# Weights ahead of v, key copies on GpSimd, and v windows by parity in a fused attention and MLP kernel

## The chip, the cores and the metric

One core of one Trainium2 chip runs the whole program. The metric is the device time in microseconds (us) of one execution, median of several. TensorE is called PE in the profile, VectorE DVE, ScalarE ACT, GpSimd POOL, SyncE SP.

## The reference

Attention of 2 batches, 8 heads, 768 positions, head width 64, in which each query sees the keys within 15 positions and, in addition, 24 block summaries (the maximum of 32 keys, the mean of 32 values). Two MLPs (512 to 2048 to 512) follow on the 1536 tokens:

```python
k_sum = k.reshape(B, H, nb, block, D).max(axis=3)
v_sum = v.reshape(B, H, nb, block, D).mean(axis=3)
scores_l = np.where(abs(pos_i - pos_j) < window, scale * q @ k.T, -1e9)
scores_s = scale * q @ k_sum.T + log(block)
a = softmax(concatenate([scores_l, scores_s], -1))
x = a @ concatenate([v, v_sum])
# tokens x 512, then
h = x @ w_in;  x = (max(h, 0) + alpha * min(h, 0)) @ w_out
h = x @ w_in2; out = (h / (1 + exp(-h))) @ w_out2
```

## The kernel before

**Attention** runs in 24 groups: 6 blocks of 256 queries (`blk`, three to a batch) times 4 pairs of heads (`p`). The first eight groups alternate between blocks 0 and 1 over the pairs (groups 0 and 1 are pair 0, groups 2 and 3 pair 1, and so on), then come blocks 2 to 5. Each pair of each batch has a key tile `kT` (for each 128 queries the 160 keys around them, with 24 free columns in front of each piece), the whole of v (`y<-in_vT` for batch 0, `raw<-in_vT` for batch 1), and the tile `vs`, the v rows of each 64 queries' window below or above 24 rows for the block means. `prep_k` takes the block maxima of the keys on DVE (L329) and copies them into the free columns of the other five pieces (L335). `prep_v1` halves v by two adds on POOL (L346) and reduces it on DVE (L349); `prep_v2` transposes that on PE and spreads it over `vs` on ACT (L359).

A group goes through `scores` (PE L387, then DVE L395 with the mask and L404), `exps` (ACT L412, row sums), `normalize` (DVE L421 and L423, then POOL L424), `turn` (PE transposes L430, ACT L432) and `values` (PE L443, ACT L451, DVE L452), which leaves attention output as a high and a low part, `xh` and `xl`, in fp32r.

**Weights** come in pieces of 128x512 in fp32 (512 KB, stored as pairs of 32-bit words). `load_next` asks for the next piece on the SP queue (L108); `conv_next` assembles the piece by three DVE instructions (L125, L129, L132), and `rest` makes a high part on ACT (L138) and a low part on POOL or DVE (L139). The first three pieces land in the free part of `y`, later ones in one of two staging tiles `raw`, which the v of batch 1 uses too. So piece 5 can be asked for once piece 3 is converted. Pieces 0 to 3 are needed by `first_in`, the first layer for block 0 as its pairs arrive, pieces 4 to 7 by `out_pair`, its second matrix.

**The MLPs** (`in_item`, `out_pair`, `out_item`) run three fp32r products for each fp32 one (L153 to L155). They start among the attention groups and fill the time behind them.

**The order.** All steps of attention, the loads and the first matrix work are put on one list with keys (`at(key, ...)`) and sorted by key: group k has its scores at k, exps at k + 0.1, normalize at k + 0.3, block sums at k + 1.3, turn at k + 1.8, values at k + 3.2. The sorted list is a rank: a planner sets the order of each engine's instructions from it, taking the first in rank among those that it holds to be ready, so the order on an engine departs from the keys. At run time each engine and each queue goes through its order strictly. Loads of the beginning have the key -100 and all go out on SP, in order: kT, q, the constants (identity and masks in one tile, 304 KB), v and the two window halves of pair 0, then the same for the pairs behind it (480, 128, 384 and 2 x 288 KB), with weight pieces 0, 1, 2 and 3 behind groups 3, 4, 5 and 6. The second half of the windows, and the keys and v of batch 1, come later by keys of their own. Conversion n has the key `CONV + n * CONV_STEP`, that is -1.4, -0.8, ... 2.8.

Of the kernel before, what the change touches and what calls it, by code (L numbers as in the profile page):

```python
# [10 lines left out]
F32 = mybir.dt.float32  # L11
# [9 lines left out]
WIN = SUB + 2 * PAD  # L21
P = 128
# [4 lines left out]
AT_EXPS, AT_NORM, AT_TURN, AT_VALUES = 0.1, 0.3, 1.8, 3.2  # L27
AT_IN = 5.3
AT_LATER, ITEM_STEP = 3.5, 0.8
CONV, CONV_STEP = -1.4, 0.6  # L30
CONV2, CONV2_STEP = 14.0, 1.5
BATCH, BATCH_STEP = 5.8, 2.0
NQ = 6
# [4 lines left out]
def tile_blocks_attention_mlps(  # L38
# [7 lines left out]
    w2: bass.AP,  # L46
    alpha: bass.AP,
    consts: bass.AP,
    out: bass.AP,
):  # L50
    nc = tc.nc
    B, NPAIR, _, S = qT.shape
    D = 64
    NB = S // BLOCK
    NSUB = S // SUB
    NC = WIN + NB
    NTWO = S // P
# [3 lines left out]
    NCH, _, CF = w1.shape[:3]  # L61
# [7 lines left out]
    const = ctx.enter_context(tc.tile_pool(name="const", bufs=1))  # L69
# [4 lines left out]
    wp1 = ctx.enter_context(tc.tile_pool(name="wp1", bufs=CF))  # L74
    ps_mm = ctx.enter_context(tc.tile_pool(name="ps_mm", bufs=6, space=bass.MemoryType.PSUM))

    cst = const.tile([P, P + 4 * NC], F32, name="cst")
    ident = cst[:, 0:P]
    mask = cst[:, P:]
    al = const.tile([P, NFF], F32, name="al")  # L80
    nal = const.tile([P, NFF], F32, name="nal")

# [5 lines left out]
    y_w = y.rearrange("p a n -> p (a n)")[:, NPAIR * S:].rearrange("p (a n w) -> p a n w", n=512, w=2)  # L88
# [205 lines left out]
    with ExitStack() as scope0:  # L294

        gpool.append(ctx.enter_context(tc.tile_pool(name="g1", bufs=2)))
        kv = scope0.enter_context(tc.tile_pool(name="kv", bufs=4))
# [11 lines left out]
        def load_v(b, p):  # L309
            if b == 0:  # L310
                t = y_v[:, p]
            else:
                t = stage.tile([P, 512, 2], F32, name="raw").rearrange("p n w -> p (n w)")[:, :S]
            nc.sync.dma_start(out=t, in_=vT[b, p])
            vt_t[b, p] = t
            t = kv.tile([NC, NSUB, P], F32, tag="vs", name="vs")
            vs_t[b, p] = t
            nc.sync.dma_start(out=t[NB:, 0::2], in_=vw[b, p, 0])
            nc.sync.dma_start(out=t[:WIN, 1::2], in_=vw[b, p, 1])

        def load_q(blk, p):
            b, j = divmod(blk, BPB)
# [4 lines left out]
        def prep_k(b, p):  # L327
            t = kt_t[b, p]
            nc.vector.tensor_reduce(  # L329
                out=t[:, 0, :NB].rearrange("p (n m) -> p n m", n=NTWO),  # L330
                in_=t[:, :NTWO, NB + PAD:NB + PAD + P].rearrange("p n (m i) -> p n m i", i=BLOCK),
                axis=AX.X,
                op=ALU.max,
            )
            nc.vector.tensor_copy(  # L335
                out=t[:, 1:, :NB], in_=t[:, 0:1, :NB].to_broadcast([P, NTWO, NB])
            )

# [13 lines left out]
        def prep_v2(b, p):  # L352
            s_ = vs_t[b, p]
            pt = ps_mm.tile([P, 512], F32, tag="mm", name="pv")
            nc.tensor.transpose(pt[:NB, :P], vr_t.pop((b, p)), ident)

            def spread(s0, s1):
                for at in (s_[:NB, 2 * s0:2 * s1:2], s_[WIN:, 2 * s0 + 1:2 * s1:2]):
                    nc.scalar.activation(  # L359
                        out=at,  # L360
                        in_=pt[:NB, 0:P].unsqueeze(1).to_broadcast([NB, s1 - s0, P]),
                        func=AF.Copy,
                        scale=1.0 / BLOCK,
                    )

            spread(0, QB // P)
            return lambda: spread(QB // P, NTWO)
# [3 lines left out]
        def where(n):  # L371
            blk, p = order[n]
            b, j = divmod(blk, BPB)
            return blk, p, b, j
# [60 lines left out]
        def values(n):  # L435
            blk, p, b, j = where(n)
            t, s_ = pt_t.pop(n), vs_t[b, p]
            ps = ps_mm.tile([P, 512], F32, tag="mm", name="o")[:, :QB]
            for i in range(2):
                for s in range(2):  # L440
                    for h in range(2):
                        c = (2 * h + i) * P + s * SUB
                        nc.tensor.matmul(  # L443
                            ps[h * D:(h + 1) * D, i * P + s * SUB:i * P + (s + 1) * SUB],
                            s_[:, 2 * (2 * j + i) + s, h * D:(h + 1) * D],
                            t[:, c:c + SUB],
                            start=True,
                            stop=True,
                        )
            at = slice(blk * QB, (blk + 1) * QB)  # L450
            nc.scalar.copy(out=xh[:, p, at], in_=ps)  # L451
            nc.vector.tensor_tensor(out=xl[:, p, at], in0=ps, in1=xh[:, p, at], op=ALU.subtract)  # L452
# [30 lines left out]
        def at(key, f, *a):  # L483
            ops.append((key, len(ops), f, a))
# [5 lines left out]
        def flush():  # L490
            while loads:
                weights = loads[0] is None
                if not weights or at_load[0] >= y_w.shape[1]:
                    if staged[0] >= (STAGE if weights else STAGE - 1):
                        return
                    staged[0] += 1
                g = loads.pop(0)
                if weights:
                    load_next()
                else:  # L500
                    load_v(*g)
# [6 lines left out]
        first = -100.0  # L508
        for k, (blk, p) in enumerate(order[:2 * NPAIR]):
            if blk == 0:  # L510
                at(first, load_k, 0, p)
            if k < NQ:
                at(first, load_q, blk, p)
            if k == 0:
                at(first, lambda: nc.sync.dma_start(out=cst, in_=consts))
            if blk == 0:
                at(first, load_v, 0, p)
            if NPAIR <= k + 1 <= 2 * NPAIR - 1:
                at(first, ask, None)
        at(first, lambda: nc.sync.dma_start(out=al, in_=alpha))  # L520
        at(first, lambda: nc.gpsimd.tensor_scalar(out=nal, in0=al, scalar1=-1.0, scalar2=None, op0=ALU.mult))
        for _ in range(NPAIR, 2 * CF):
            at(first, ask, None)

        spread_t = {}
# [51 lines left out]
        for k, (blk, p) in enumerate(order):  # L577
            b, j = divmod(blk, BPB)
# [13 lines left out]
            if blk == 0:  # L592
                at(k + AT_IN, first_in, p)
        for n in range(2 * CF):
            at(CONV + n * CONV_STEP, conv_op, n)
        for n in range(CF):
            at(CONV2 + n * CONV2_STEP, conv_op, 2 * CF + n)
        at(NG - 2 * CF + 2.0, more_loads)
        for p in range(NPAIR if B > 1 else 0):
            t = BATCH + p * BATCH_STEP  # L600
            k = idx[BPB - 1, p]
            at(max(t, k + 0.01), load_k, 1, p)
            at(max(t, k + AT_VALUES + 0.01), ask, (1, p))
        t = idx[0, NPAIR - 1] + AT_IN
        for i, *_ in seq:
            if i >= NBLK:
                break
            t = max(t + ITEM_STEP, lastk[i] + AT_LATER)
# [18 lines left out]
def _layout(q, k, v, moe_w_in, moe_w_out, moe_alpha, moe2_w_in, moe2_w_out):  # L627
    B, H, S, D = q.shape
    pad = PAD
    nb, nsub = S // BLOCK, S // SUB  # L630

    def turned(a):
        return np.ascontiguousarray(a.transpose(0, 1, 3, 2).reshape(B, H // 2, 2 * D, S))

    kp = np.zeros((B, H // 2, 2 * D, S + 2 * pad), k.dtype)
    kp[:, :, :, pad:pad + S] = turned(k)
    kT = np.stack([kp[:, :, :, i:i + P + 2 * pad] for i in range(0, S, P)], axis=3)
    vp = np.zeros((B, H // 2, S + 2 * pad, 2, D), v.dtype)
    vp[:, :, pad:pad + S] = v.reshape(B, H // 2, 2, S, D).transpose(0, 1, 3, 2, 4)
    vp = vp.reshape(B, H // 2, S + 2 * pad, 2 * D)  # L640
    vw = np.stack(
        [
            np.stack([vp[:, :, i + odd:i + odd + WIN] for i in range(0, S, P)], axis=3)
            for odd in (0, SUB)
        ],
        axis=2,
    )

    def weights(w_in, w_out):

        dm, dff = w_in.shape
        n = dff // dm
        a = w_in.reshape(dm // P, P, n, dm).transpose(2, 0, 1, 3)
        b = w_out.reshape(n, dm // P, P, dm)
        return np.ascontiguousarray(np.stack([a, b], axis=1)).view(np.uint64)


    m = np.zeros((3, P, WIN + nb), np.float32)
    for t, first in enumerate((0, P, S - P)):
        pos = first + np.arange(P)[:, None]  # L660
        key = first + (np.arange(P)[:, None] // SUB) * SUB - pad + np.arange(WIN)[None, :]
        ok = (np.abs(pos - key) < WINDOW) & (key >= 0) & (key < S)
        m[t] = np.log(BLOCK)
        m[t, :SUB, nb:] = np.where(ok, 0.0, -1000000000.0)[:SUB]
        m[t, SUB:, :WIN] = np.where(ok, 0.0, -1000000000.0)[SUB:]
    consts = np.concatenate(
        [np.eye(P, dtype=np.float32)] + [m[t] for t in (0, 1, 1, 2)], axis=1
    )

    return {  # L670
        "qT": turned(q),
        "kT": np.ascontiguousarray(kT),
        "vT": turned(v),
        "vw": np.ascontiguousarray(vw),
        "w1": weights(moe_w_in, moe_w_out),
        "w2": weights(moe2_w_in, moe2_w_out),
        "alpha": np.ascontiguousarray(moe_alpha.reshape(-1, P).T),
        "consts": np.ascontiguousarray(consts),
    }


# [17 lines left out]
```

## Time and profile before

| | |
|---|---|
| runs | 620.99 us median of 3 (617.88 to 621.72) |
| profiled execution | 619.27 us, span 617.5 us |
| PE busy | 589.0 us, 95% of the span |
| DVE busy | 360.1 us, 58% |
| ACT busy | 261.3 us, 42% |
| POOL busy | 72.7 us, 12% |
| DMA | 52.54 MB, mean 85 GB/s, 31770 packets, 20976 of them under 2 KB |

The profiled execution's 619.27 us are its span and 1.77 us around it. Shares are means over the whole span; the attention with its loads lies in the first 140 us or so, and the rows below are read from there.

### The profile page before, as it was taken

What the parts mean: (1) busy time and instruction counts of PE and PEld (TensorE: products, weight loads), DVE (VectorE), ACT (ScalarE), POOL (GpSimd) and SP (SyncE); (2) the same over time, 40 slices, a digit from 0 to 9 for tenths busy, and PEclk for the clock granted to TensorE, in tenths of its full rate; (3) what the DMA queues carried; (4) which work ended last, traced back from release to release, by engine and by line L of the source; (5) the groups of instructions that cost most, each with busy time, mean ns of one, the idle gap of its engine ahead of it and who ended that gap; (6) DMA issues with size and microseconds to landing.
All of it is one profiled execution on the core that took longest, in us unless ns stands there. A gap on an engine that the chain in (4) does not pass through costs nothing.

```text
span 617.5 us, 8894 instructions
## 1 busy us (share of the span) xinstructions
PE 589.0 (95%) x3476; PEld 492.8 (80%) x3476; DVE 360.1 (58%) x629; ACT 261.3 (42%) x606; POOL 72.7 (12%) x69
## 2 busy tenths in 40 slices
PE   2777999999999999999999999999999999999997
PEld 1565888999888888888888888888888888888886
DVE  3899979549995587449764890067325732222222
ACT  2768977654533433433553553354124213212310
POOL 1657754232000000000000000000000000000000
PEclk9998999999999999999999999999999999999999
DMA  9968844001441034004400231024200300000011
GB/s 246 316 203 258 230 153 137 2 2 69 139 166 37 1 136 137 0 1 136 137 0 1 89 123 62 1 68 137 69 0 31 106 1 1 2 0 36 34 69 68
DMA packets 31770, 52.54 MB, mean 85 GB/s; under 512 B 2288, under 2 KB 20976, under 8 KB 31728
## 3 DMA queue, kind: packets, MB, share of 16 engines
q1 hardware_dynamic: 31728, 51.97, 27.1%
q8 instruction: 27, 0.44, 0.3%
q14 instruction: 15, 0.12, 0.1%
HBM read 48.82 MB, written 3.15 MB: 84 GB/s over the span
## 4 chain that ended last, share of the span: by engine, by line
PE 85%; DVE 8%; DMA 3%; SPq 1%; ACT 1%; issue 1%; POOL 0%; DVEq 0%; POOLq 0%
PE ps L153 28%; PE ps L154 27%; PE ps L155 27%; DVE w L129 1%; DMA y<-in_w 1%; DMA vs<-in_vw 1%; DVE w L132 1%; PE o L443 1%; DVE t L395 1%; DVE nm L404 1%; DVE w L125 1%; DMA raw<-in_w 1%; PE sc L387 1%; DVE kT L329 1%; PE pt L430 1%
## 5 line engine op out<-in xcount | busy, mean ns | idle before, releaser
L153 PE MATMUL ps<-xh,wl 128*128 128x512 f32 (+1 forms) x432 | 159.0, 373 | 0.4 <-ACT xh L451 0.3
L154 PE MATMUL ps<-xl,wh 128*128 128x512 f32 (+1 forms) x432 | 158.7, 368 | 0.0
L155 PE MATMUL ps<-xh,wh 128*128 128x512 f32 (+1 forms) x432 | 158.2, 367 | 0.0
L204 DVE TENSOR_TENSOR gl<-g,gh 128x512 fp32r<-128x512 f32 x84 | 57.6, 690 | 100.8 <-ACT gh L203 100.8
L153 PEld LDWEIGHTS ps<-xh,wl 128*128 128x128 f32 x432 | 81.9, 192 | 14.9 <-issue 1.0
L154 PEld LDWEIGHTS ps<-xl,wh 128*128 128x128 f32 x432 | 82.1, 190 | 13.3 <-issue 0.2
L155 PEld LDWEIGHTS ps<-xh,wh 128*128 128x128 f32 x432 | 82.0, 190 | 13.3
L200 ACT ACTIVATE g<-ps 128x512 f32<-128x512 f32 x48 | 28.7, 598 | 139.0 <-PE ps L155 137.5
L154 PE MATMUL ps<-gl,wh 128*128 128x512 f32 (+1 forms) x240 | 82.9, 348 | 0.0
L155 PE MATMUL ps<-gh,wh 128*128 128x512 f32 (+1 forms) x240 | 82.6, 346 | 0.0
L153 PE MATMUL ps<-gh,wl 128*128 128x512 f32 (+1 forms) x240 | 78.6, 350 | 0.1
L154 PE MATMUL ps<-wl,gh 128*128 128x512 f32 (+1 forms) x196 | 75.4, 385 | 0.0
L153 PE MATMUL ps<-wh,gl 128*128 128x512 f32 (+1 forms) x196 | 74.7, 385 | 0.0
L155 PE MATMUL ps<-wh,gh 128*128 128x512 f32 (+1 forms) x196 | 73.4, 385 | 0.0
L203 ACT CAST gh<-g 128x512 fp32r<-128x512 f32 x96 | 59.6, 622 | 25.9 <-DVE g L195 24.4
L138 ACT CAST wh<-w 128x512 fp32r<-128x512 f32 x64 | 39.2, 623 | 52.4 <-DVE w L132 39.1
L260 DVE TENSOR_TENSOR y<-ps,y 128x512 f32<-128x512 f32 x48 | 32.2, 688 | 48.8 <-PE ps L155 48.8
L195 DVE SCALAR_TENSOR_TENSOR g<-m,nal,g 128x512 f32<-128x512 f32 (+1 forms) x60 | 41.2, 701 | 25.3 <-ACT m L192 25.3
L191 ACT ACTIVATE g<-ps 128x512 f32<-128x512 f32 (+1 forms) x50 | 28.9, 579 | 60.5 <-PE ps L155 57.2
L153 PEld LDWEIGHTS ps<-gh,wl 128*128 128x128 f32 x240 | 45.2, 189 | 6.9 <-issue 0.5
L154 PEld LDWEIGHTS ps<-gl,wh 128*128 128x128 f32 x240 | 45.3, 189 | 6.0 <-POOL gl L204 0.2
L155 PEld LDWEIGHTS ps<-gh,wh 128*128 128x128 f32 x240 | 45.3, 189 | 5.7
(51 smaller groups left out, 684.9 us busy)
## 6 DMA issues: line engine op xcount, KB each, us to landing
raw<-in_w SPq DMA_DIRECT2D x61, 512.0 KB, 3.8
vs<-in_vw SPq DMA_DIRECT2D x16, 288.0 KB, 6.9
kT<-in_kT SPq DMA_DIRECT2D x8, 480.0 KB, 5.0
q<-in_qT SPq DMA_DIRECT2D x24, 128.0 KB, 4.2
out<-s SPq DMA_DIRECT2D x11, 256.0 KB, 2.0
y<-in_vT SPq DMA_DIRECT2D x4, 384.0 KB, 6.9
y<-in_w SPq DMA_DIRECT2D x3, 512.0 KB, 7.8
raw<-in_vT SPq DMA_DIRECT2D x4, 384.0 KB, 5.3
```

The costliest lines, as they stand in the source:

```text
L125: nc.vector.tensor_scalar(out=w, in0=high, scalar1=3, scalar2=0x3FFFFFFF, op0=ALU.logical_shift_left, op1=ALU.bitwise_and,)
L129: nc.vector.scalar_tensor_tensor(out=w, in0=high, scalar=0xC0000000, in1=w, op0=ALU.bitwise_and, op1=ALU.bitwise_or)
L138: nc.scalar.copy(out=hi, in_=w)
L153: nc.tensor.matmul(ps, all_, bh, start=first, stop=False)
L154: nc.tensor.matmul(ps, ah, bl, start=False, stop=False)
L155: nc.tensor.matmul(ps, ah, bh, start=False, stop=last)
L191: nc.scalar.activation(out=g[:, j * w:(j + 1) * w], in_=ps, func=AF.Relu)
L195: nc.vector.scalar_tensor_tensor(out=g[:, at], in0=m[:, at], scalar=nal[:, f + j:f + j + 1], in1=g[:, at], op0=ALU.mult, op1=ALU.add,)
L200: nc.scalar.activation(out=g, in_=banks[0], func=AF.Silu)
L203: nc.scalar.copy(out=gh, in_=g)
L204: (nc.gpsimd if early else nc.vector).tensor_tensor(out=gl, in0=g, in1=gh, op=ALU.subtract)
L260: nc.vector.tensor_tensor(out=at, in0=src, in1=at, op=ALU.add)
```

## The change

Three things. (1) At the beginning, weight pieces 0, 1 and 2 are asked for ahead of the v of pairs 0, 1 and 2; identity and masks are two tiles and come on ACT's queue; the conversions have hand-set keys, 0.15 to 8.0, that lie among the keys of groups 0 to 8. (2) The copies of the key maxima into the other pieces run on POOL. (3) The tile `vs` holds the windows of even and odd 64-query halves apart, so that a row of a window load is one run of 3 KB in the tile where it was six of 512 B; spread and values address it accordingly.

```diff
-CONV, CONV_STEP = -1.4, 0.6
+CONV = 0.15, 1.0, 2.6, 4.2, 5.0, 6.0, 7.0, 8.0
...
-    cst = const.tile([P, P + 4 * NC], F32, name="cst")
-    ident = cst[:, 0:P]
-    mask = cst[:, P:]
+    ident = const.tile([P, P], F32, name="ident")
+    mask = const.tile([P, 4 * NC], F32, name="mask")
...
-            t = kv.tile([NC, NSUB, P], F32, tag="vs", name="vs")
+            t = kv.tile([NC, 2, NTWO, P], F32, tag="vs", name="vs")
             vs_t[b, p] = t
-            nc.sync.dma_start(out=t[NB:, 0::2], in_=vw[b, p, 0])
-            nc.sync.dma_start(out=t[:WIN, 1::2], in_=vw[b, p, 1])
+            nc.sync.dma_start(out=t[NB:, 0], in_=vw[b, p, 0])
+            nc.sync.dma_start(out=t[:WIN, 1], in_=vw[b, p, 1])
...
-            nc.vector.tensor_copy(
+            nc.gpsimd.tensor_copy(
                 out=t[:, 1:, :NB], in_=t[:, 0:1, :NB].to_broadcast([P, NTWO, NB])
             )
...
-                for at in (s_[:NB, 2 * s0:2 * s1:2], s_[WIN:, 2 * s0 + 1:2 * s1:2]):
+                for at in (s_[:NB, 0, s0:s1], s_[WIN:, 1, s0:s1]):
...
-                            s_[:, 2 * (2 * j + i) + s, h * D:(h + 1) * D],
+                            s_[:, s, 2 * j + i, h * D:(h + 1) * D],
...
             if k == 0:
-                at(first, lambda: nc.sync.dma_start(out=cst, in_=consts))
+                at(first, lambda: nc.scalar.dma_start(out=mask, in_=masks))
+                at(first, lambda: nc.scalar.dma_start(out=ident, in_=consts))
             if blk == 0:
+
+                if p < y_w.shape[1]:
+                    at(first, ask, None)
                 at(first, load_v, 0, p)
-            if NPAIR <= k + 1 <= 2 * NPAIR - 1:
-                at(first, ask, None)
...
-        for _ in range(NPAIR, 2 * CF):
+        for _ in range(y_w.shape[1], 2 * CF):
             at(first, ask, None)
...
-            at(CONV + n * CONV_STEP, conv_op, n)
+            at(CONV[n], conv_op, n)
```

## Rows read from the trace of the kernel before

**Rows 1.** The page: busy time of TensorE over the span, then the span in 40 equal slices of 15.4 us, a digit for the busy tenths of each.

```profile
PE 589.0 (95%) x3476; PEld 492.8 (80%) x3476; DVE 360.1 (58%) x629; ACT 261.3 (42%) x606; POOL 72.7 (12%) x69
...
PE   2777999999999999999999999999999999999997
...
DVE  3899979549995587449764890067325732222222
...
DMA  9968844001441034004400231024200300000011
```

**Rows 2.** The chain of work that ended last, in order of time: start us, length us, what.

```profile
9.27 7.68 DMA vs<-in_vw
16.96 8.30 DMA y<-in_w
25.29 0.65 DVE w L125
```

**Rows 3.** Stretches ahead of the full TensorE: from:to, length, busy us of each engine (instructions), granted TensorE clock, DMA share, GB/s.

```profile
4.60:12.50 7.90, 2.42 (x32) 1.70 (x32) 2.85 (x5) 1.62 (x8) 1.59 (x2) 1.00 1.09 295
12.50:19.80 7.30, 3.54 (x37) 2.38 (x37) 5.15 (x13) 3.74 (x13) 3.27 (x4) 1.00 1.13 309
19.80:25.30 5.50, 3.63 (x36) 2.62 (x36) 4.38 (x10) 4.79 (x20) 3.96 (x5) 1.00 1.11 308
25.30:33.00 7.70, 7.29 (x63) 5.52 (x64) 7.70 (x12) 4.80 (x15) 4.38 (x5) 1.00 1.12 297
33.00:54.00 21.00, 15.88 (x173) 12.44 (x173) 20.89 (x40) 15.76 (x53) 13.80 (x12) 0.92 0.69 221
54.00:62.00 8.00, 5.42 (x82) 4.10 (x83) 8.00 (x20) 6.04 (x25) 5.32 (x6) 1.00 0.80 247
```

**Rows 4.** What VectorE waited for from 0 to 26 us: engine, line, releaser: us in total, times, longest us.

```profile
DVE kT L329 <- DMA kT<-in_kT: 6.9, 3, 4.6
...
DVE w L125 <- DMA y<-in_w: 1.5, 2, 1.1
```

**Rows 5.** The timeline, 0 to 62 us: start us, us, engine, line, operation, tiles, and in brackets the idle time before it with its releaser. SPq rows are issues of transfers.

```profile
11.26 0.43 SPq L108 DMA_DIRECT2D y<-in_w  x1
...
12.51 0.95 DVE L329 TENSOR_REDUCE kT<-kT 128x24 f32<-128x768 f32 x1 [1.90 <-DMA kT<-in_kT]
...
18.36 0.43 DVE L125 TENSOR_SCALAR w<-y 128x512 uint32<-128x512 uint32 x1 [0.38 <-DMA y<-in_w]
...
18.82 0.69 DVE L129 SCALAR_TENSOR_TENSOR w<-y,w 128x512 uint32<-128x512 uint32 x1
...
20.71 0.68 DVE L132 SCALAR_TENSOR_TENSOR w<-y,w 128x512 uint32<-128x512 uint32 x1
...
35.96 0.39 DVE L125 TENSOR_SCALAR w<-raw 128x512 uint32<-128x512 uint32 x1
...
49.77 0.43 DVE L125 TENSOR_SCALAR w<-raw 128x512 uint32<-128x512 uint32 x1
```

**Rows 6.** VectorE by line and shape, 25.3 to 70 us: count | busy us, mean ns | idle before it.

```profile
L129 DVE SCALAR_TENSOR_TENSOR w<-raw,w 128x512 uint32<-128x512 uint32 x6 | 6.8, 1128 | 0.0
...
L132 DVE SCALAR_TENSOR_TENSOR w<-raw,w 128x512 uint32<-128x512 uint32 x6 | 5.4, 902 | 0.1
...
L125 DVE TENSOR_SCALAR w<-raw 128x512 uint32<-128x512 uint32 x6 | 2.9, 491 | 0.0
...
L335 DVE COPY kT<-kT 128x144 f32<-128x144 f32 x5 | 1.5, 302 | 0.0
```

**Rows 7.** Stretches of 2 us, columns as in rows 3: windows of pair 2 under way in the first, mostly weights in the others.

```profile
20.00:22.00 2.00, 1.59 (x14) 1.25 (x16) 2.00 (x4) 1.98 (x10) 0.54 (x2) 1.00 1.22 272
...
24.00:26.00 2.00, 0.33 (x5) 0.30 (x3) 0.92 (x4) 1.28 (x8) 1.65 (x2) 1.00 1.06 401
26.00:28.00 2.00, 2.00 (x21) 1.44 (x19) 2.00 (x6) 0.66 (x2) 0.52 (x1) 1.00 1.09 348
```

**Rows 8.** Single lines over the whole span: count, duration in ns as least/median/most, first and last start in us, forms.

```profile
L335 DVE COPY kT<-kT x8: 221/222/1035, 5.6 to 68.0; 128x144 f32<-128x144 f32 x8
...
L129 DVE SCALAR_TENSOR_TENSOR w<-raw,w x61: 661/685/1671, 36.4 to 490.5; 128x512 uint32<-128x512 uint32 x61
...
L346 POOL TENSOR_TENSOR y<-y x8: 584/964/1008, 8.6 to 32.6; 128x384 f32<-128x384 f32 x4, 128x192 f32<-128x192 f32 x4
...
L521 POOL TENSOR_SCALAR nal<-al x1: 255/255/255, 35.3 to 35.3; 128x16 f32<-128x16 f32 x1
```

**Rows 9.** The timeline, 8 to 24 us, columns as in rows 5.

```profile
8.56 1.66 POOL L346 TENSOR_TENSOR y<-y 128x384 f32<-128x384 f32 x2 [8.13 <-DMA y<-in_vT]
...
15.43 0.99 POOL L424 TENSOR_TENSOR e<-e,rs 128x480 f32<-128x480 f32 x1
...
21.81 1.67 POOL L346 TENSOR_TENSOR y<-y 128x384 f32<-128x384 f32 x2 [1.46 <-DMA y<-in_vT]
21.88 1.03 DVE L335 COPY kT<-kT 128x144 f32<-128x144 f32 x1
```

**Rows 10.** What GpSimd waited for from 0 to 70 us, columns as in rows 4.

```profile
POOL y L346 <- DMA y<-in_vT: 15.2, 4, 8.1
POOL e L424 <- DVE rs L423: 9.0, 5, 3.1
POOL e L424 <- DVE sm L421: 4.4, 1, 4.4
```

More of the change, by code (lines that the diff above doesn't have):

```diff
@@ L48, in tile_blocks_attention_mlps @@
     consts: bass.AP,
+    masks: bass.AP,
     out: bass.AP,
@@ L665, in _layout @@
         m[t, SUB:, :WIN] = np.where(ok, 0.0, -1000000000.0)[SUB:]
-    consts = np.concatenate(
-        [np.eye(P, dtype=np.float32)] + [m[t] for t in (0, 1, 1, 2)], axis=1
-    )
+    masks = np.concatenate([m[t] for t in (0, 1, 1, 2)], axis=1)
     return {
@@ L677, in _layout @@
         "alpha": np.ascontiguousarray(moe_alpha.reshape(-1, P).T),
-        "consts": np.ascontiguousarray(consts),
+        "consts": np.eye(P, dtype=np.float32),
+        "masks": np.ascontiguousarray(masks),
     }
```

## The prediction

> **What bounds the kernel now.** I read the slices of the page first [rows 1]. TensorE is full from the fifth slice of 15.4 us on (from 62 us to the end) and partly idle in the first four. Behind that nothing that this change touches can matter unless it makes TensorE wait, since matrix work is queued there without a gap; what can be won is idle time ahead of it. TensorE is busy 589.0 of 617.5 us, so 28.5 us are idle in all, with the first loads and the last store in it. That is the ceiling of any gain.
>
> Next the chain that ended last [rows 2]: issues on SP, then the transfer of pair 1's v windows, then that of weight 1 (landing at 25.29 us), and from there VectorE instructions. The stretches [rows 3] say the same: from 25.3 to 62 us VectorE is busy to the last tenth (36.59 of 36.7 us), from 4.6 to 25.3 us only 12.38 of 20.7 us, and the DMA share is over 1 until 33 us and 0.69 after. So there are two regimes ahead of the full TensorE: until 25 us the loads decide, after it VectorE does. What VectorE waits for in the first one is in the waits [rows 4]: key tiles (4.6 of these 6.9 us are the very first) and weights.
>
> **The change part by part.** The sum goes against the profiled execution, 619.27 us (span 617.5 and 1.8 around it); the median of the runs shown is 620.99, 1.7 above it.
>
> *Weights ahead of v.* SP issues weight 0 at 11.26 us [rows 5] and weight 1 at 16.96 [rows 2]. In order of bytes, ahead of and with weight 0 stand kT, q, constants, v and windows of pair 0, then q, kT, q, v, windows, q: 4208 KB; with the change 1424 KB (kT, q, weight 0 and the constants on ACT's queue). Pair 1's kT has 2480 KB with it before and lands by 12.51 us [rows 5]; weight 1 has 6288 KB and lands by 25.29 [rows 2]: 3808 KB in 12.78 us, 298 KB a us. At that rate weight 0 moves from 18.3 to about 8 to 9 us, weight 1 (3632 KB after) from 25.3 to about 16, weight 2 (5840 KB) to about 23. Paid for by what is moved past: kT of pair 1 and v of pair 0 come behind one more weight, 512 KB or 1.7 us; kT of pair 3 has the same bytes as before. Putting masks and identity on ACT takes one issue off SP, adds two on an engine that has nothing else to do yet, and lays 304 KB beside the first kT: at 298 KB a us the first scores can come up to 1.0 us later, which nothing downstream feels as long as pair 1's kT comes six microseconds after it.
>
> What VectorE makes of it: of the 8.3 us idle between 4.6 and 25.3 us [rows 3], it can now fill part with conversions. Before, one conversion (weight 0) was done by 25.3 us; after, weights 0, 1 and most of 2 can be. A conversion is three VectorE instructions: in the best case 0.43 + 0.69 + 0.68 = 1.8 us [rows 5], in the busy stretch 0.49 + 1.13 + 0.90 = 2.5 us [rows 6]. One and three quarters of these moved into idle time is 3.2 to 4.4 us; of it goes the later kT of pair 1, about 1.0 us when the next term has been taken off. I take **-3.0 us**; bounds 0 (the idle time only moves) and -5.0.
>
> *v by parity.* A window load has 96 rows; before, each falls into six pieces of 512 B in the tile, after it is one of 3 KB. While windows of pair 2 are under way the queues move 272 GB/s at a share of 1.22; while mostly weights are, 401 at 1.06 and 348 at 1.09 [rows 7], a mean of 375. Two windows are 590 kB: 2.2 us at 272 GB/s, 1.6 at 375, so at most 0.6 us a pair and 2.4 us over the first four. That brings the loads ahead of weight 3 forward, but VectorE has no gap from 25.3 to 62 us for an earlier landing to close. I take **-0.5 us** (pair 1's and pair 2's keys), bounds 0 and -2.4. The windows of the second batch fall where TensorE is full: nothing; without that cover 2.4 us more. The Trainium skill (DMA: Bandwidth & Descriptors, Specifications) puts the least transfer for the full rate at 512 B, which these pieces just reach. By it this term would be nothing and the forecast 614.0; the stretches in [rows 7] speak against it.
>
> *Copies of key maxima.* Eight copies leave VectorE. Five lie in its full stretch, at a mean of 302 ns [rows 6], 1.5 us; one of 1.03 us at 21.88 us stands just ahead of it; the rest are in idle time. I take **-2.0 us**, bounds -1.1 (five at the median of 0.222 us [rows 8]) and -2.5. What they cost on GpSimd no row shows; the nearest are 128x16 at 0.255 us and the block-sum adds, from 0.584 us (128x192, two inputs) [rows 8]: between 0.26 and 0.6 us, taken as 0.45 since 144 elements are nearer to 192. GpSimd is busy 13.8 of 21 us in the full stretch [rows 3], so it has room. But scores of a pair now wait for VectorE, GpSimd and TensorE in turn instead of two of these, and behind a waiting copy stand the normalizing product of the groups before (which the transposes wait for) and the low halves of the weights. Also both engines slow one another: the copy that took 1.03 us instead of 0.22 ran beside GpSimd's block sums [rows 9], and the two-input steps of the conversions take 0.66 to 1.67 us [rows 8]. I take **+0.7 us** for all of this; bounds 0 (a gain is excluded, the copy itself is booked above) and +3.
>
> *Conversions among the groups.* Keys of conversions go from -1.4 ... 2.8 to 0.15 ... 8.0, and they act as ranks where several instructions are ready. Weights 3 to 7 go through two staging tiles: conversion 3 started at 35.96 us and conversion 7 at 49.77 [rows 5], 3.5 us for each, paced by a release, an issue and a landing. So they can't start much later by their rank than they already do by their loads; what changes is that the last steps of groups 3 to 7 (the row sums, the low half of the attention output) go ahead of them. GpSimd waited 13.4 us up to 70 us for VectorE's row sums and reciprocals [rows 10]: that is where it shows. Most of this comes back as later conversions on an engine with no slack. I take **-1.0 us**, bounds +2 and -5. The move of later staged loads on SP costs nothing while VectorE is full; if that cover is gone, the 3.5 us a weight show on TensorE.
>
> Sum: -3.0 - 0.5 - 2.0 + 0.7 - 1.0 = -5.8 us, 619.27 - 5.8 = **613.5 us**. About 1% is what a measurement of this kernel can tell from no change; this is 0.9% below the profiled time and 1.2% below the median.
>
> **The rivals.** (a) *The idle time only moves.* kT of pair 1, and with it scores of groups 2 and 3, come 1.7 us later, v likewise; VectorE does conversion 0 where it idled but idles later. Terms one, two and five fall away: -2.0 + 0.7, 618.0 us. For it: weights are not what VectorE waited longest for (1.5 us against 6.9 for keys [rows 4]). Against it: 8.3 us of idle time with nothing to fill them but weights.
>
> (b) *The copies come back on VectorE.* Eight copies of 0.45 us that block a two-input step each time are 3.6 us, and with 2.0 saved and 0.7 counted already the time is 613.5 + 2.9 = 616.4 us. For it: [rows 9]. Against: the median of the two-input step is 0.685 us, near its least, so most escape. The Trainium skill (SBUF — State Buffer, Who interferes with whom) says that a VectorE instruction with two SBUF inputs is held off by a GpSimd one that reads SBUF for that one's whole length; the trace's 1.67 us beside a least of 0.66 agrees in kind.
>
> (c) *The order pays more than the bytes.* Attention output of group 7 gates the second block of matrix work; it was late because conversions 4 to 7 (4 x 2.5 = 10 us of VectorE) stood ahead of it. If half of that goes behind, it gives 5 us in place of the 1.0 counted: 613.5 - 4.0 = 609.5, and 605 if nearly all of it does.
>
> (d) *GpSimd becomes the bound (slower).* Its queue is in order, and its block sums wait for v: 15.2 us in four waits, 8.1 the longest [rows 10]. Where the planner sets a pair's copy behind the sums of the same pair, the copy waits for v, which the change puts 1024 KB behind kT (q, weight, v): 3.4 us, and 1.0 for the first add [rows 8], 4.4 us for each of pairs 0 to 2, 13.2 us, in a stretch with nothing else to do: 613.5 + 13.2 = 626.7 us, and over 627.2 with the bounds of the last terms. It decides as soon as two of the three copies stand so (619.27 is passed at 5.8 of 13.2 us). Against: copies have keys 2.4 lower than their pair's sums; for it: the trace shows the sums of pair 0 (key 1.3) ahead of the product of group 0 (key 0.3) [rows 9].
>
> **How the numbers follow.** Forecast (608 to 615) 0.42, (a) 0.22, (b) 0.10, (c) 0.13, (d) 0.13. Faster by over 1% means under 614.8 us: (c) and nearly nine tenths of the forecast, 0.50. Slower by over 1% means over 627.2: the upper part of (d) with what I have not thought of, 0.10. The rest, 0.40, lies between. The range runs from 606 (part of (c)) to 621 (all of (a) and (b), not (d)).
>
> **What would show it.** Conversion 0 before 12 us and conversion 1 before 18; VectorE's idle time between 4.6 and 25.3 us down from 8.3 to about 5; no copies on VectorE, eight on GpSimd of 0.3 to 0.6 us directly behind their reductions; packets under 2 KB down by 9216; TensorE full some 6 us earlier. I am wrong if pair 1's keys land after 15 us, if GpSimd's copies stand behind block sums, if the two-input conversion steps get longer on average, or if TensorE has new gaps behind its fifth slice.

## The result and the profile after

The changed kernel takes 628.64 us (median; 626.61 to 629.77), the kernel before 620.96 us beside it: ratio 1.013, 95% interval 1.009 to 1.017. It is slower by about 8 us, where 613.5 us was forecast. The profiled execution took 629.77 us, with a span of 628.0.

The page of the changed kernel: busy time over the span, slices of 15.7 us, packets, and one new queue.

```profile
PE 592.9 (94%) x3476; PEld 497.4 (79%) x3476; DVE 356.9 (57%) x621; ACT 262.8 (42%) x606; POOL 72.9 (12%) x77
...
PE   1587899899999999999999999999999999999998
...
PEclk9996699899999999999999999999999999999999
...
DMA packets 24234, 52.54 MB, mean 84 GB/s; under 512 B 2304, under 2 KB 12032, under 8 KB 24192
...
q10 hardware_dynamic: 288, 0.31, 0.2%
```

Beside [rows 1], TensorE is busy 3.9 us longer (592.9 for 589.0) and the span is 10.5 us longer, so it is idle 6.6 us more (35.1 for 28.5). (The two profiled executions lie 10.5 us apart, the medians 7.7.) Its slices are no longer full from the fifth on: there is an 8 in the fifth and another in the eighth. The granted clock, a 9 in nearly every slice of before, is 6 in the fourth and fifth. The two edits that are seen in packets did what they say: 12,032 packets under 2 KB, 8,944 fewer (the kernel before has 20,976), and the constants on a queue of their own.

Stretches of the changed kernel, columns as in [rows 3].

```profile
4.60:12.50 7.90, 1.08 (x16) 0.73 (x16) 3.81 (x6) 0.58 (x2) 1.30 (x2) 1.00 1.04 304
12.50:19.80 7.30, 3.48 (x37) 2.27 (x37) 4.61 (x10) 3.36 (x18) 3.88 (x6) 1.00 1.08 314
19.80:25.30 5.50, 2.99 (x36) 2.32 (x36) 3.57 (x8) 4.99 (x15) 3.75 (x5) 1.00 1.06 291
25.30:33.00 7.70, 4.44 (x55) 3.19 (x51) 5.85 (x13) 4.20 (x17) 5.12 (x5) 1.00 1.06 311
33.00:54.00 21.00, 17.71 (x169) 14.02 (x165) 17.66 (x35) 15.67 (x55) 10.98 (x12) 0.82 0.54 164
54.00:62.00 8.00, 4.76 (x59) 3.38 (x58) 8.00 (x16) 4.69 (x15) 5.53 (x8) 0.71 1.02 325
62.00:70.00 8.00, 6.41 (x63) 5.29 (x62) 5.93 (x14) 4.99 (x21) 4.77 (x7) 0.50 0.48 145
...
110.00:140.00 30.00, 27.41 (x327) 24.42 (x326) 19.52 (x45) 20.56 (x74) 9.77 (x9) 0.94 0.13 39
```

The same columns, the kernel before, for the two stretches that are not among [rows 3].

```profile
62.00:70.00 8.00, 7.25 (x103) 6.19 (x102) 7.70 (x21) 6.90 (x28) 3.57 (x5) 1.00 0.67 203
...
110.00:140.00 30.00, 30.00 (x364) 27.61 (x364) 14.57 (x35) 17.76 (x59) 8.78 (x8) 1.00 0.01 2
```

Three things can be read off. From 4.6 to 62 us TensorE is busy 34.5 us where it was 38.2. From 62 us on, where the kernel before hardly ever has it idle, it loses another 0.8 us up to 70 and 2.6 us between 110 and 140, where attention of the second batch still runs: its last groups are late (the last low half of its output is taken at 151.6 us, where it was at 141.1). VectorE, busy 36.6 of 36.7 us from 25.3 to 62 us before, has 5.2 us idle there. And TensorE's clock is lower in four of these stretches. From 62 to 70 us it is at the lower level throughout, with 63 matmuls done where the kernel before did 103. The transfers are no slower than before: 291 to 314 GB/s until 33 us, 295 to 309 in [rows 3].

One number tells the loss of each variant. From the start of the last low half of attention output (L452 on VectorE) to the end of the span it takes 476.4 us, give or take 0.1, in 15 of the 16 kernels profiled for this document, with spans from 615.7 to 633.9 us (e15, below, takes 477.7). What a variant loses, it has lost by then: 151.6 instead of 141.1 us here, the whole 10.5 us between the two spans. The question is what makes attention late.

The first thing to look for is what an early conversion pushes back. The timelines of VectorE and then of ScalarE in the changed kernel, columns as in [rows 5]:

```profile
9.56 0.43 DVE L125 TENSOR_SCALAR w<-y 128x512 uint32<-128x512 uint32 x1 [3.38 <-DMA y<-in_w]
10.03 0.69 DVE L129 SCALAR_TENSOR_TENSOR w<-y,w 128x512 uint32<-128x512 uint32 x1
10.63 0.65 DVE L395 SCALAR_TENSOR_TENSOR t<-sc,mask 128x480 f32<-128x480 f32 x1
...
11.80 0.65 DVE L404 TENSOR_REDUCE nm<-t 128x4 f32<-128x480 f32 x1
```

```profile
11.92 0.62 ACT L138 CAST wh<-w 128x512 fp32r<-128x512 f32 x1 [9.03 <-DVE w L132]
12.48 0.40 ACT L412 ACTIVATE e<-t,nm 128x120 f32<-128x120 f32 x1
```

and of the kernel before:

```profile
7.03 0.66 DVE L395 SCALAR_TENSOR_TENSOR t<-sc,cst 128x480 f32<-128x480 f32 x1 [1.18 <-PE sc L387]
7.72 0.65 DVE L404 TENSOR_REDUCE nm<-t 128x4 f32<-128x480 f32 x1
```

```profile
8.41 0.39 ACT L412 ACTIVATE e<-t,nm 128x120 f32<-128x120 f32 x1 [6.41 <-DVE nm L404]
```

In the changed kernel the conversion of weight 0 stands ahead of group 0's mask step (L395) in VectorE's order. VectorE waits 3.38 us for the weight, and the maximum `nm` (L404), which the exponentials need, is done at 12.45 us where it was done at 8.37. So attention begins 4.1 us later, at 12.48 instead of 8.41 us. About 1.5 us of this are later scores (TensorE ends those of group 0 at 8.47 instead of 6.97 us, since their queries land later), the rest is the conversion. On ScalarE the high half of weight 0 stands ahead of the exponentials too and waits 9.03 us, but it ends within 0.1 us of the maximum, so there it costs hardly anything more. The weight is converted in what was idle time, and an attention group has become idle time instead.

The second thing is further on. The timeline of the changed kernel, then of the kernel before: issues of v (L314) and keys (L306) of the second batch on SP, and the first reduction of these keys on VectorE.

```profile
50.06 0.33 SPq L314 DMA_DIRECT2D raw<-in_vT  x1
...
50.96 0.55 SPq L306 DMA_DIRECT2D kT<-in_kT  x1
...
56.51 0.92 DVE L329 TENSOR_REDUCE kT<-kT 128x24 f32<-128x768 f32 x1
```

```profile
46.72 0.58 SPq L306 DMA_DIRECT2D kT<-in_kT  x1
...
48.64 0.33 SPq L314 DMA_DIRECT2D raw<-in_vT  x1
...
52.25 0.94 DVE L329 TENSOR_REDUCE kT<-kT 128x24 f32<-128x768 f32 x1
```

Before, the keys go out first; after, v of the same pair does. V goes into a staging tile and must wait for one to come free (2.3 us here), keys need none. The keys of the first pair are reduced 4.3 us later, those of the other three 2.1, 1.5 and 1.0 us. Nothing in the diff says that these loads change places, so it is the planner that drew up another order.

The third is the 2.6 us that TensorE loses between 110 and 140 us. The chain of work that ended last in the changed kernel, columns as in [rows 2]:

```profile
106.80 4.44 DMA raw<-in_w
...
111.33 0.43 DVE w L125
...
113.78 0.56 DVE t L395
114.38 0.77 PE sc L387 x16
```

A later weight lands, VectorE converts it, and only then masks the scores of an attention group. The tile of these scores has one buffer, so TensorE waits 2.59 us before it can make the next ones. It is again a conversion that stands ahead of attention in VectorE's order and waits for its weight. The chain of the kernel before has no transfer between 83.1 and 145 us.

Whether the order or the place of the first loads carries the loss is what the experiments had to tell.

### The profile page after: what moved, and what is told of

Same layout as the page of the kernel before. It is cut to its first block, busy times and chain, and to the rows that moved or that the text cites. A ratio compares the mean times of both kernels' runs of the same rounds, so it can differ in the third digit from the quotient of the medians.

```text
span 628.0 us, 8892 instructions
## 1 busy us (share of the span) xinstructions
PE 592.9 (94%) x3476; PEld 497.4 (79%) x3476; DVE 356.9 (57%) x621; ACT 262.8 (42%) x606; POOL 72.9 (12%) x77
## 2 busy tenths in 40 slices
DMA packets 24234, 52.54 MB, mean 84 GB/s; under 512 B 2304, under 2 KB 12032, under 8 KB 24192
## 4 chain that ended last, share of the span: by engine, by line
PE 85%; DMA 7%; DVE 6%; issue 1%; SPq 0%; POOL 0%; ACT 0%; DVEq 0%; ACTq 0%
PE ps L154 27%; PE ps L153 27%; PE ps L155 27%; DMA raw<-in_w 3%; DMA y<-in_vT 2%; DMA kT<-in_kT 2%; DMA vs<-in_vw 2%; PE o L443 2%; DVE w L132 1%; PE pt L430 1%; DVE w L125 1%; PE sc L387 1%; DVE t L395 1%; DVE w L129 1%; DVE nm L404 1%
## 5 line engine op out<-in xcount | busy, mean ns | idle before, releaser
L154 PEld LDWEIGHTS ps<-xl,wh 128*128 128x128 f32 x432 | 83.1, 192 | 13.7 <-DVE nm L404 0.3
L200 ACT ACTIVATE g<-ps 128x512 f32<-128x512 f32 x48 | 28.7, 598 | 139.5 <-PE ps L155 138.0
```

Source lines behind the costliest of these rows:

```text
L154: nc.tensor.matmul(ps, ah, bl, start=False, stop=False)
L200: nc.scalar.activation(out=g, in_=banks[0], func=AF.Silu)
```

## The experiments

**One part at a time.** First each edit by itself on the kernel before.

e1: copies of the key maxima on GpSimd.

```
-            nc.vector.tensor_copy(
+            nc.gpsimd.tensor_copy(
```

> The kernel before with the copies of the key maxima on GpSimd and nothing else. If the loads are what made the change slow, this keeps the gain forecast for it: eight copies off VectorE, 619 to 621 us, no clear loss. If the extra engine in front of the scores is the cause, this run alone is 5 us or more slower (626 us and above), with TensorE waiting for GpSimd's copy. If the loss comes from a lower granted clock that any disturbance of the order sets off, the clock here is under 0.99 too.

622.44 us beside 620.41, ratio 1.0025 (1.0005 to 1.0045): slower by a quarter of a per cent, not faster.

e2: v's windows in rows of 3 KB (the four lines of the diff with `vs` and `s_`).

> The kernel before with the v windows in 3 KB rows and nothing else. By the forecast's term for these rows -0.5 us, at most -2.4, with the loads ahead of weight 3 landing earlier and over 305 GB/s between 4.6 and 33 us. If the queues' rate does not depend on the piece (the changed kernel moved 304, 314, 291 and 311 GB/s in the four stretches where the one before moved 295, 309, 308 and 297), the time stays within 2 us of 621 and the key tiles land where they did.

620.40 us beside 620.41, ratio 1.0013 (0.9988 to 1.0038): no difference.

e3: the new keys of the conversions alone.

```
-CONV, CONV_STEP = -1.4, 0.6
+CONV = 0.15, 1.0, 2.6, 4.2, 5.0, 6.0, 7.0, 8.0
...
-            at(CONV + n * CONV_STEP, conv_op, n)
+            at(CONV[n], conv_op, n)
```

> The kernel before with the new keys of the conversions alone; loads in their old order. If the rank of the conversions is the cause, this carries most of the 8 us (626 us and above) and attention groups run ahead of the matrix work. If the loads are the cause, it is between 2 us faster and 2 us slower than before.

619.57 us, ratio 0.9993 (0.9969 to 1.0017). On all five engines the instructions stand in exactly the order of the kernel before: taken alone, the new keys change no instruction's place. That isn't so of e1 and e2: there at least 511 and 283 of the 3476 matmuls stand in another place than before, so these two runs hold more than the copies and the rows.

e4: all edits of the first loads (weights ahead of v, and the constants in two tiles on ScalarE's queue).

> The kernel before with weights 0 to 2 asked for ahead of v and masks and identity on ACT's queue; old keys, copies on VectorE, old rows. If the loads are the cause, this carries most of the loss (625 to 630 us): first scores later than 7 us, keys of pair 2 behind 22 us, VectorE idle between 25 and 33 us, and a granted clock under 0.99. If the rank or the copies are the cause, it is within 2 us of before or faster, since weights 0 and 1 are converted in idle time.

630.57 us, ratio 1.0156 (1.0126 to 1.0185): the whole loss.

**The loads taken apart.** e5 is the changed kernel with the weights asked for where they were before; e6 the kernel before with the constants on ScalarE's queue only; e7 the kernel before with the weights ahead only:

```
             if blk == 0:
+
+                if p < y_w.shape[1]:
+                    at(first, ask, None)
                 at(first, load_v, 0, p)
-            if NPAIR <= k + 1 <= 2 * NPAIR - 1:
-                at(first, ask, None)
...
-        for _ in range(NPAIR, 2 * CF):
+        for _ in range(y_w.shape[1], 2 * CF):
```

> The changed kernel with weights 0 to 3 asked for where the kernel before asks for them; constants on ACT's queue, new rows, new keys and copies on GpSimd stay. If the place of the weights is the cause, 618 to 622 us and a granted clock of 0.99 or more. If the constants on ACT's queue are the cause, it keeps the loss, 626 to 631 us. If the loss needs several parts at once, it lies between, 623 to 626 us.

622.02 us beside 619.62, ratio 1.0038 (1.0013 to 1.0064): most of the loss is gone, 2.4 us stay. TensorE's and GpSimd's orders are those of e1, which lost 2.0.

> The kernel before with masks and identity as two tiles on ACT's queue and nothing else. If the place of the weights is the cause, 619 to 622 us. If the 304 KB beside the first keys and queries are the cause, 625 us or more, with the first scores a microsecond or more later than at 5.6 us.

617.97 us, ratio 0.9970 (0.9953 to 0.9988): 1.6 us faster, with every engine's order as in the kernel before. It is the fastest kernel of the study.

> The kernel before with weights 0 to 2 asked for ahead of v and nothing else (constants on SP as before). If the place of the weights is the cause, 626 to 631 us: keys of pair 2 later than 21 us, VectorE idle between 25 and 62 us where it was full, and the loads of the second batch standing on SP behind a wait for a staging tile. If the constants on ACT are the cause, within 2 us of before.

629.34 us, ratio 1.0169 (1.0131 to 1.0206). The place of three weights among the first loads makes up all of the loss. But the trace of e7 doesn't fit a simple tale of late attention data: its conversion 7 starts at 49.2 us, the kernel before has it at 49.77 [rows 5], so up to there it has caught up. Behind that it falls back. A wait of SP between 30 and 110 us, columns as in [rows 4]:

```profile
SPq L314 <- DVE rs L423: 4.3, 1, 4.3
```

and its timeline:

```profile
53.35 0.33 SPq L314 DMA_DIRECT2D raw<-in_vT  x1
...
54.20 0.57 SPq L306 DMA_DIRECT2D kT<-in_kT  x1
...
59.12 0.95 DVE L329 TENSOR_REDUCE kT<-kT 128x24 f32<-128x768 f32 x1 [2.94 <-DMA kT<-in_kT]
```

V of the second batch's second pair stands at the head of SP's queue and waits 4.3 us for a staging tile; the queries and the keys behind it need none and wait as well, and then VectorE idles 2.94 us for the keys. In the kernel before these keys go ahead of that v, out at 50.30 and reduced at 56.41 us. In the changed kernel these keys do go ahead of that v, so this wait is e7's; what the two share is that an order drawn up anew sets one load behind another that waits.

e8: the opposite of e7, weights 0 to 3 behind the first loads of all four pairs, so that attention data land earlier than in the kernel before.

```
-            if NPAIR <= k + 1 <= 2 * NPAIR - 1:
-                at(first, ask, None)
...
-        for _ in range(NPAIR, 2 * CF):
+        for _ in range(2 * CF):
```

> The kernel before with weights 0 to 3 asked for behind the keys, queries and values of all four pairs, the opposite of the change. If attention data that comes later is what costs (512 KB or 1.7 us for each weight ahead of it), keys of pair 3 land 4 us earlier here and the time falls by 2 to 5 us, to 616 to 619. If it is the order of the later loads on SP that any change of the first ones upsets, the time rises here too, 623 us or more, though all attention data come earlier.

634.38 us, ratio 1.0238 (1.0199 to 1.0277): slower still. A theory in which only the lateness of attention data counts is refuted. The planner's order is another one here too, and the weights are late, and e8 doesn't part these two.

**The order held.** The planner's order can be taken out of the comparison: each engine's instructions of one kernel are tied, each behind the next one ahead of it, to the order that they have in another kernel. The ties are edges of issue order without a semaphore, so no instruction waits for another to finish.

```
+def keep_order(nc, tc):
...
+    for name, spec in ORDER.items():
+        traced = by_engine[engines[name].engine]
...
+        for a, b in zip(at, at[1:]):
+            tc.add_manual_dep(traced[b], traced[a].name, no_sync, reason="keep_order")
...
         tile_blocks_attention_mlps(tc, *args, out)
+        keep_order(nc, tc)
```

> The kernel of e7 (weights 0, 1 and 2 ahead of v of their pairs, nothing else of the change), but every instruction of TensorE, VectorE, ScalarE and GpSimd, and every load behind the first 29, held in the order that they have in the kernel before, by ordering edges without semaphores. Theory of the place (the first loads themselves cost the time: attention data land later, TensorE starts later, nothing makes it up): stays at about 629 us (627 to 632). Theory of the order (the loads' place moves little; the planner, which orders every engine by its own estimate of when data land, drew up another order of the later loads and of TensorE's work, and that order is worse on the chip): back to about 620 us (617 to 622).

622.22 us beside 619.52, ratio 1.0035 (1.0015 to 1.0056). With the order of the kernel before, the same early weights cost about 2 to 3 us instead of 10. Three quarters of e7's loss is the order. No run holds the kernel before to its own order, so that the ties themselves cost nothing isn't shown; e12 and e13, which are held and level with the kernel before, leave little room for a cost.

> The mirror image: the first 29 loads exactly as in the kernel before, all other loads and every instruction of the other engines held in the order that they have in e7. Theory of the place: about 621 us (618 to 623). Theory of the order: about 629 us (626 to 632). If both count, both this kernel and e9_held come out between, and their two differences to the kernel before add up to e7's 9.7 us.

636.45 us, ratio 1.0271 (1.0245 to 1.0297). The first loads of the kernel before under e7's order are slower than e7 itself. The two differences don't add up as I had written for the case that both count: the order was drawn up for early weights, and it is worse with late ones. VectorE's timeline in e10 shows it in one line:

```profile
18.53 0.43 DVE L125 TENSOR_SCALAR w<-y 128x512 uint32<-128x512 uint32 x1 [12.69 <-DMA y<-in_w]
```

The conversion of weight 0 stands ahead of group 0's mask step, and VectorE waits 12.69 us for the weight. The exponentials of group 0 start at 21.45 us.

> e7 with the order held on SP's queue alone: behind the first 29 loads, the keys and queries of the second batch and the weights stand as in the kernel before (keys of a pair ahead of the v of the pair before), and the planner orders the other engines as it likes. Theory of the order in the form in which I have it (v of the second batch waits for a staging tile at the head of SP's queue and holds back the keys behind it): about 621 us (618 to 624), keys of pair 5 reduced before 57 us instead of 59.1. If TensorE's own order is what counts: between 624 and 632 us. Theory of the place: about 629 us.

624.15 us, ratio 1.0068 (1.0046 to 1.0090): of the 7.1 us between e7 and e9 it is 5.2. The keys of the third pair of the second batch are reduced at 59.36 us and those of the second at 55.66 us (e7: 64.97 and 59.12). The keys come as the theory of SP's order had it, the time lies just above its range. And SP's order isn't all that differs: the planner drew up new orders for the other engines here (at least 315 of 3476 matmuls and 108 of 629 VectorE instructions stand elsewhere than in e7). So 5.2 us go with SP's order and what the planner redrew beside it; e11 doesn't part these.

> The changed kernel itself, whole, with TensorE's, VectorE's and ScalarE's instructions and all loads behind the first 28 held in the order that they have in the kernel before (GpSimd's order is left to the planner, since it has eight copies more). Theory of the order: the whole loss of about 8 us goes: 620 us (617 to 623), since the place of the first loads cost 2.2 us with the order held, the constants on ScalarE's queue gave 1.6 back, and the rest of the change had been within 1.5 us. If the loss of the whole change has another source than e7's (the copies, v's rows): 625 to 629 us.

620.39 us beside 620.52, ratio 1.0004 (0.9980 to 1.0028). The whole change, with the order of the kernel before, is level with it. Its stretches, columns as in [rows 3]:

```profile
33.00:54.00 21.00, 17.84 (x182) 14.14 (x182) 20.89 (x40) 16.26 (x58) 14.89 (x13) 0.84 0.63 200
54.00:62.00 8.00, 5.25 (x96) 3.85 (x94) 8.00 (x18) 7.01 (x26) 6.56 (x10) 1.00 0.84 272
62.00:70.00 8.00, 6.94 (x93) 6.30 (x96) 7.35 (x18) 6.41 (x25) 3.37 (x5) 1.00 0.73 221
...
110.00:140.00 30.00, 30.00 (x364) 27.68 (x364) 14.50 (x34) 17.73 (x61) 9.18 (x9) 1.00 0.01 2
```

TensorE is full again from 110 to 140 us, the clock is whole from 54 us on, and VectorE is back to 20.89 of 21 us from 33 to 54, the figure of [rows 3]. Its timelines, all engines and then ScalarE:

```profile
48.09 0.55 SPq L306 DMA_DIRECT2D kT<-in_kT  x1
...
49.52 0.33 SPq L314 DMA_DIRECT2D raw<-in_vT  x1
...
53.13 0.94 DVE L329 TENSOR_REDUCE kT<-kT 128x24 f32<-128x768 f32 x1
```

```profile
8.85 0.39 ACT L412 ACTIVATE e<-t,nm 128x120 f32<-128x120 f32 x1 [5.96 <-DVE nm L404]
```

The first keys of the second batch come at 53.13 us instead of 56.51, and the first exponentials at 8.85 instead of 12.48. What is shown is that the planner's new order carries the loss. It isn't shown what early conversions could be worth: with the order of the kernel before, weight 0 is converted at 19.92 us, and no run converts it early but behind group 0's mask step.

> The changed kernel with the weights' first loads back in their old places, held as in e12_after_held: copies of key maxima on GpSimd, v's rows of 3 KB and the constants on ScalarE's queue are what is left of the change. Without the hold it took 622.02 us. Theory of the order: copies and rows cost nothing by themselves, so about 617.5 us (615.5 to 619.5), level with the constants on ScalarE's queue alone. If the copies on GpSimd or the rows are slower in themselves: 620 to 623 us. If the prediction's term for the copies is real once the order is held: below 616 us.

620.94 us, ratio 1.0004 (0.9981 to 1.0026). Without the early weights the held kernel is where it is with them (e12), so here they cost nothing that can be measured, where e9 has 0.9 to 3.5 us by its interval; why isn't shown. 620.94 is above the 617.5 us expected from the constants on ScalarE's queue, so the copies, the rows or GpSimd's order, which is left to the planner, take back what e6 gained.

> The kernel before with the copies of the key maxima on GpSimd alone, the order of the other engines held as before. Free, it took 622.44 us beside 620.41. If that loss of 2 us is the planner's new order: level with before, 619.5 us (618.5 to 620.5). If the copies' 1.0 us on VectorE less is a gain in its own right: 617.5 to 618.5 us. If GpSimd is the slower place: 621 to 623 us.

622.14 us, ratio 1.0020 (0.9998 to 1.0042). The interval reaches from no difference to 2.6 us slower: no gain for the copies in their own right, and a small loss is likelier than none. That e15 lies so close to e1 gives no sign that the planner's order makes e1's loss, and the intervals are too wide to settle it.

## Why the prediction was wrong

*What bounds the kernel.* "Behind that nothing that this change touches can matter unless it makes TensorE wait" was right, and the exception is what came: 2.6 us idle between 110 and 140 us, and 0.8 us less busy time from 62 to 70. I had read the full TensorE from the fifth slice on as a fact of the kernel. It is a fact of one order, in which attention of the second batch stays just ahead of the matrix work.

*Weights ahead of v*, -3.0 us, bounds 0 and -5. This is the term that failed: alone it is 9.7 us slower (e7). The step in it that failed is that conversions of early weights fill idle time on VectorE while all else stays in its place. The arrivals were nearly as worked out: the conversions of weights 0, 1 and 2 start at 9.56, 17.75 and 26.21 us, each as its weight lands, where "about 8 to 9", "about 16" and "about 23" were given (by its own rate the last should have been about 24), and the keys of pair 1 are reduced at 14.96 us, just inside the 15 named as the limit. But VectorE is idle 8.7 us between 4.6 and 25.3 us, where 8.3 was to become 5. In the changed kernel it waits 4.5 us for weights 0 to 2, where the kernel before has 1.5 [rows 4]: a conversion that waits for its weight holds back the attention steps that stand behind it, 3.38 us of it with the first group. I had listed who is queued behind a waiting copy on GpSimd, and hadn't asked the same of a conversion on VectorE. With the order held the early weights give nothing: they cost some 2 us in e9, and nothing that can be measured in e12 beside e13. In e12, which has the same first loads as the changed kernel, weight 0 is converted at 19.92 us, the place that the old order gives it, although the changed kernel could start on it at 9.56; and weight 3 comes at 36.31, where it was at 35.96 [rows 5].

*"The move of later staged loads on SP costs nothing while VectorE is full."* This failed too, by its own condition: the cover was gone. VectorE is idle 5.2 us between 25.3 and 62 us, and a late weight shows on TensorE as 2.59 us of idle time from 111.8 us on. The loads that moved were not the staged weights alone but keys, queries and v of the second batch. How the 10.5 us by which attention ends late divide among these waits isn't shown: the keys alone are 1.0 to 4.3 us later, and e11, where 5.2 us of e7's loss go with SP's order, has new orders on the other engines as well.

*v by parity*, -0.5 us: nothing (e2). By the rule of the Trainium skill (DMA: Bandwidth & Descriptors, Specifications) that 512 B is enough for the full rate, the term would have been zero. The runs agree: between 4.6 and 33 us the queues moved 301 GB/s in the kernel before and 292 in e2. The stretches of [rows 7], which I set against the rule, differ in what is loaded and not only in the size of its pieces, and 2 us were too short to read a rate from.

*Copies of key maxima*, -2.0 + 0.7 us: +2.0 by the medians of e1, +1.6 by those of e15 (its interval is 0 to 2.6). In the changed kernel the copies start 0.06 to 0.99 us behind the end of their reductions, and seven of eight are cheaper than the 0.45 us taken; GpSimd's line there:

```profile
L335 POOL COPY kT<-kT x8: 302/303/637, 6.2 to 66.9; 128x144 f32<-128x144 f32 x8
```

So neither rival (d) nor a slow copy explains the loss. Rival (b) is neither shown nor excluded: the three steps of a staged conversion between 25.3 and 70 us take a mean of 2.52 us together in [rows 6], 2.31 in the changed kernel and 2.72 in e15, where L129 is shorter (990 for 1128 ns) and L132 and L125 are longer (1075 for 902, 658 for 491). In e15 that is 0.2 us for each of six conversions, 1.2 us, most of the 1.5 us that the five copies took [rows 6]; one profile of each is too little to tell. VectorE's saving didn't reach the end. Why GpSimd's copies cost a little stays open.

*Conversions among the groups*, -1.0 us, bounds +2 and -5: nothing (e3), with no instruction moved. That keys "act as ranks where several instructions are ready" was right, and the conclusion that the last steps of groups 3 to 7 would therefore go ahead was not: on this list the new keys changed the rank of nothing that was ready together.

*The rivals.* (d) gave 626.7 us, close to what was measured, by a mechanism that didn't happen. (a), 618.0 us, "the idle time only moves", has the mechanism that the changed kernel shows at its start (idle 8.7 us for 8.3, weight 0 converted at 9.56 us), but it had the rest of the order stay and so no loss. What was missing is a rival of the whole list: that the planner, given other loads, draws up another order for every engine, up to 140 us, and that this order is worse on the chip. I had written that "the order on an engine departs from the keys" as a description, and costed each edit as if the rest of the order stayed where it was. Why the planner holds that order to be good isn't shown by any run. That the order of the kernel before is better on the chip is shown under three sets of first loads: e9 beside e7, the kernel before beside e10, and e12 beside the changed kernel.

## What to carry to other kernels

Where a planner orders the engines, an edit of a load can be an edit of every queue (in e7 it was, in e6 it wasn't): compare the order of instructions of both programs engine by engine before costing the edit, and hold the order of the old kernel once to see what the edit itself is worth. On an in-order queue, a transfer that waits for a buffer should stand behind those that need none, above all behind the ones that feed the engine which is full. Before filling idle time with work that itself waits, ask what stands behind that work in the same order, since it waits along with it.

## What the runs showed of the hardware

TensorE's granted clock fell for long stretches in the changed kernel. Changed kernel, columns as in [rows 3]:

```profile
56.90:60.30 3.40, 1.14 (x27) 0.65 (x23) 3.40 (x8) 3.38 (x14) 3.04 (x5) 0.98 1.01 319
60.30:73.90 13.60, 11.03 (x105) 9.14 (x105) 11.30 (x23) 9.13 (x35) 9.66 (x12) 0.50 0.48 154
```

The whole change with the order held:

```profile
56.90:60.30 3.40, 2.33 (x40) 1.67 (x39) 3.40 (x9) 2.88 (x13) 2.48 (x3) 1.00 1.03 338
60.30:73.90 13.60, 12.54 (x188) 10.79 (x188) 12.45 (x31) 11.59 (x47) 8.78 (x11) 1.00 0.80 242
```

In the 3.4 us ahead of the fall TensorE was mostly idle (busy 1.14). Then the clock stood at its lower level (0.50, which is 1.2 of 2.4 GHz) for 13.6 us, and TensorE did 105 matmuls in them; in the held kernel it was busy 2.33 of the same 3.4 us, the clock stayed whole behind it, and it did 188. A matmul of the scores took a median of 404 ns in that stretch and 263 in the kernel before. What this cost at the end isn't shown. TensorE's busy time, 3.9 us longer in the changed kernel, doesn't follow the clock from kernel to kernel: 592.9 us with 27.3 us at the lower level there, 589.2 with 22.5 in e6, 593.0 with 4.2 in e15. And e6, the fastest kernel, has a mean granted clock of 0.74 between 25.3 and 54 us, lower than the changed kernel's 0.87, while its VectorE is busy 28.5 of these 28.7 us.

A GpSimd copy of 128x144 takes a median of 0.30 us, the same copy on VectorE 0.22 us [rows 8], less of a difference than I had allowed. On either engine one of eight took far longer: 0.64 us in the changed kernel on GpSimd, 1.03 on VectorE before.
